# One switch and a new hand-written order in a chunk-attention and token-mixing kernel: every transpose of x and u on TensorE

## The chip, the cores and the metric

The kernel runs on one core of one Trainium2 chip. The metric is device time in microseconds (us), the median of several runs. One core has five engines with queues of their own: TensorE (PE, matmuls; PEld are its weight loads), VectorE (DVE), ScalarE (ACT), GpSimd (POOL) and SyncE (SP). In this kernel POOL computes almost nothing: it issues DMAs, and so does SP.

## The reference

```python
# q, k, v: (8 batches, 8 heads, 576 tokens, 64), float32
scores = q_chunk @ k_chunk.T / sqrt(64)          # 9 chunks of 64 tokens, each on its own
attn   = softmax(scores)
x      = attn @ v_chunk                          # -> (8, 576, 512), heads side by side

theta  = x @ w_theta                             # 512 x 512
zr, zi = x * cos(theta), x * sin(theta)
y      = w_tok_r @ zr + w_tok_i @ zi             # 576 x 576, over the tokens of a batch
u      = x + y
out    = u + relu(u @ w_ch)                      # 512 x 512
```

## The kernel before

The 8 batches are taken in 4 pairs (p = 0 to 3). The 1152 tokens of a pair are 9 tiles of 128 (the middle one takes 64 tokens of each batch), and for attention these are 5 groups g of 2, 2, 1, 2 and 2 tiles. Groups 0 and 1 belong to the pair's first batch, 3 and 4 to its second, group 2 to both. Work is cut into steps, and a list written out by hand, `ORDER`, says in which order the steps are emitted. Each engine and each DMA queue runs its own instructions strictly in that order, so a step whose input is late holds up everything behind it on its engine. The steps, with p and g or another index behind the dot, and after the colon bits that choose engines:

- Loads, all issued from POOL: `lq` (q and k of a group, one DMA of 256 KB each, L165), `lv` (v, 2 or 3 DMAs, L186), `lw` and `lc` (w_theta, w_ch, L203), `lt.half.ri` (a part of a token weight, L194 and L199).
- `a1`: 32 PE transposes of q and k (L277) and two copies out of PSUM, one behind the other (L208 on DVE, L210 on ACT). `a2`: scores (L303) and their exponential on ACT (L310). `a3`: attention times v (L331), then reciprocal and product on DVE (L338, L345); the result is x.
- `a4`: the transpose of x, which `a5` needs. Below bit 16 it is 8 PE transposes (4 for the middle group, L385) and a copy out of PSUM; with bit 16 it is DMA transposes issued from SP (L364, L360).
- `a5`: theta (L410, 8 matmuls, 4 for the middle group), then cos and sin on ACT (L420, L424). `z`: x times cos or sin on DVE (L435; the middle group has four smaller products and two small DMAs, L445 to L450).
- `tw`: PE transposes of the token weights (L229). `yh` and `y`: token mixing, 18 matmuls each (L467 in quarters for the first batch of all, L488 for the others), and u = x + y on DVE (L475, L496). They leave u transposed, in `uT`.
- `w.p.j`: u @ w_ch for one of 9 tiles, 4 matmuls (L519). For the final sum u must be turned back. In the first `U_DMA` batches `w` does this with 4 more matmuls against the identity (L527), ACT takes the relu (L535) and DVE adds (L542). In the later ones step `ut` has turned u by DMA transposes from SP (L510), and one DVE instruction does relu and sum (L544).
- `st.p.j`: that DVE instruction, and the output DMA (L554) from POOL (bit 2) or SP.

PSUM results go through 4 buffers in turn, so a PE step must wait until the evacuation of the step four places earlier is done.

```python
if 2 * p + int(j >= KT) < U_DMA:        # in w (L526, L533) and in out_tile (L541)
if bits & 16:                           # in a4 (L376)
    xt(p, g)                            # dma_start_transpose on SP
```

Of the kernel before, what the change touches and what calls it, by code (L numbers as in the profile page):

```python
# [16 lines left out]


ORDER = """
lq.0.0:0 a1.0.0:2 lq.0.2:0 a1.0.2:2 lq.0.1:0 a2.0.0:0 a2.0.2:0 a1.0.1:3 lv.0.2:0  # L20
lv.0.0:0 a3.0.0.0:0 a3.0.2.0:0 a2.0.1:0 a3.0.0.1:0 lv.0.1:0 a3.0.1.0:0 lw.0:0 lq.0.3:0
a3.0.1.1:0 a4.0.0:1 a4.0.2:0 lq.0.4:0 a4.0.1:1 a5.0.2:0 lt.0.1:0 z.0.2.0:0 a5.0.0:0
lt.0.0:0 z.0.0.0:0 a1.0.3:3 a5.0.1:0 lq.1.0:0 a1.0.4:0 z.0.1.0:0 lv.0.4:0 tw.0.2:0
tw.0.0:0 z.0.1.1:0 lt.1.0:0 z.0.0.1:0 tw.0.1:0 a2.0.3:0 lt.1.1:0 a2.0.4:0 lv.0.3:0
lv.1.0:0 a1.1.0:2 yh.0.0:0 lq.1.2:0 a3.0.4.0:0 a2.1.0:0 a3.0.4.1:0 yh.0.1:0 a4.0.4:1
lc.0:0 tw.1.1:0 tw.1.2:1 tw.1.0:1 a3.0.3.0:0 lq.1.1:0 a3.0.3.1:0 a5.0.4:0 lv.1.2:0
a4.0.3:1 yh.1.0:0 lq.1.3:0 a5.0.3:0 z.0.4.0:0 lq.1.4:0 a3.1.0.0:0 z.0.3.0:0 a1.1.2:2
yh.1.1:0 z.0.3.1:0 z.0.4.1:0 a2.1.2:0 lv.1.3:0 a3.1.0.1:0 a1.1.1:3 lv.1.1:0 w.0.0:0
st.0.0:0 y.0.1.0:0 a3.1.2.0:0 a1.1.3:0 lq.2.0:0 w.0.1:0 lv.1.4:0 a4.1.2:1 st.0.1:0
y.0.1.1:0 a2.1.3:0 a1.1.4:3 a2.1.1:0 a3.1.3.0:0 lq.2.2:0 w.0.2:0 st.0.2:0 y.0.1.2:0  # L30
a2.1.4:0 a3.1.3.1:0 a4.1.0:1 a5.1.2:0 lv.3.0:0 a3.1.1.0:0 a1.2.0:2 a5.1.0:0 lq.2.1:0
lv.2.2:0 a3.1.4.0:0 lv.2.0:0 a3.1.1.1:0 y.0.1.3:0 a4.1.1:1 a3.1.4.1:0 z.1.0.0:0 a1.2.2:1
w.0.3:0 st.0.3:0 a4.1.3:1 a4.1.4:0 lq.2.3:0 z.1.2.0:0 a5.1.1:0 w.0.4:0 a5.1.4:0 st.0.4:2
w.0.5:0 lq.2.4:0 z.1.1.0:0 z.1.0.1:0 z.1.4.0:0 a5.1.3:0 st.0.5:0 z.1.1.1:0 a2.2.0:0
a1.2.1:2 y.1.0.0:0 lv.2.1:0 a1.2.3:1 a3.2.0.0:0 lv.2.4:0 z.1.3.0:0 a2.2.2:0 y.1.0.1:0
z.1.3.1:0 a2.2.1:0 lv.3.2:0 a3.2.2.0:0 a1.2.4:0 w.0.6:0 st.0.6:0 a4.2.2:1 lv.2.3:0
y.1.0.2:0 w.0.7:0 z.1.4.1:0 a3.2.0.1:0 lq.3.0:0 a2.2.4:0 st.0.7:2 lv.3.4:0 y.1.0.3:0
a3.2.1.0:0 a3.2.4.0:0 y.1.1.0:0 a4.2.0:0 a3.2.4.1:0 a1.3.0:3 a2.2.3:0 lq.3.2:0
a3.2.1.1:0 w.0.8:0 lq.3.1:0 lq.3.3:0 a5.2.2:0 a4.2.1:0 lv.3.3:0 w.1.0:0 lq.3.4:0
st.0.8:0 lv.3.1:0 z.2.2.0:0 st.1.0:0 y.1.1.1:0 a5.2.1:0 w.1.1:0 st.1.1:2 a5.2.0:0  # L40
z.2.1.0:0 z.2.0.0:0 y.1.1.2:0 a3.2.3.0:0 a1.3.2:0 z.2.1.1:0 a2.3.0:0 a1.3.1:0 z.2.0.1:0
w.1.2:0 st.1.2:0 y.1.1.3:0 y.2.0.0:0 ut.1.1.0:0 a2.3.2:0 ut.1.1.3:0 a3.3.0.0:0 a1.3.3:0
a3.2.3.1:0 y.2.0.1:0 a4.2.4:16 a4.2.3:17 a2.3.1:0 a3.3.0.1:0 a1.3.4:0 a2.3.3:0
a3.3.1.0:0 ut.1.1.2:0 y.2.0.2:0 a3.3.1.1:0 a4.3.0:17 a2.3.4:0 ut.2.0.1:0 ut.1.1.1:0
a3.3.3.0:0 a5.2.3:0 w.1.3:0 a5.2.4:0 st.1.3:2 y.2.0.3:0 z.2.3.0:0 w.1.4:0 a4.3.1:17
a5.3.0:0 z.2.3.1:0 st.1.4:2 z.2.4.0:0 z.2.4.1:0 w.1.5:0 st.1.5:2 z.3.0.0:0 a5.3.1:0
w.1.6:0 st.1.6:0 y.2.1.0:0 a3.3.4.0:0 a3.3.2.0:0 ut.2.0.0:0 ut.2.0.2:0 y.2.1.1:0
a3.3.4.1:0 a3.3.3.1:0 z.3.1.0:0 w.1.7:0 st.1.7:2 y.2.1.2:0 ut.2.0.3:0 w.1.8:0 a4.3.2:18
a5.3.2:0 a4.3.3:17 z.3.0.1:0 a4.3.4:17 st.1.8:2 w.2.0:0 st.2.0:2 z.3.2.0:0 z.3.1.1:0
y.2.1.3:0 a5.3.3:0 z.3.3.0:0 w.2.1:0 ut.2.1.1:0 ut.2.1.3:0 a5.3.4:0 st.2.1:0 w.2.2:0  # L50
ut.2.1.0:0 ut.2.1.2:0 st.2.2:2 y.3.0.0:0 w.2.3:0 st.2.3:2 y.3.0.1:0 w.2.4:0 st.2.4:2
y.3.0.2:0 z.3.3.1:0 ut.3.0.1:0 ut.3.0.2:0 ut.3.0.0:0 w.2.5:0 z.3.4.0:0 z.3.4.1:0
st.2.5:0 y.3.0.3:0 w.2.6:0 ut.3.0.3:0 st.2.6:2 y.3.1.0:0 w.2.7:0 st.2.7:0 y.3.1.1:0
w.2.8:0 st.2.8:2 ut.3.1.1:0 ut.3.1.0:0 y.3.1.2:0 w.3.0:0 st.3.0:2 y.3.1.3:0 w.3.1:0
st.3.1:2 w.3.2:0 w.3.3:0 ut.3.1.2:0 ut.3.1.3:0 w.3.4:0 st.3.2:0 st.3.3:2 st.3.4:0
w.3.5:0 st.3.5:0 w.3.6:0 st.3.6:0 w.3.7:0 w.3.8:0 st.3.7:0 st.3.8:2
""".split()


# [1 line left out]
def kernel(  # L61
# [28 lines left out]
    VP = D + 2  # L90
    NAT = 7

    U_DMA = 3

    const = ctx.enter_context(tc.tile_pool(name="const", bufs=1))
    glob = ctx.enter_context(tc.tile_pool(name="glob", bufs=1))
# [104 lines left out]
    def load_w(ap, f16):  # L201

        nc.gpsimd.dma_start(f16, ap.rearrange("(a p) e -> p a e", p=P))  # L203
# [38 lines left out]
    st = {}  # L242
# [271 lines left out]
    def w(p, j):  # L514
# [3 lines left out]
        for db in range(NDB):  # L518
# [6 lines left out]
            )  # L525
            if 2 * p + int(j >= KT) < U_DMA:  # L526
                nc.tensor.matmul(  # L527
# [4 lines left out]
        r = None  # L532
        if 2 * p + int(j >= KT) < U_DMA:  # L533
            r = outp.tile([P, DM], FP32, name="relu", bufs=3)
# [3 lines left out]
    def out_tile(p, j, bits):  # L538
        ps, r = st[p].pop(("w", j))
        o = outp.tile([P, DM], FP32, name="o32")  # L540
        if 2 * p + int(j >= KT) < U_DMA:  # L541
            nc.vector.tensor_tensor(out=o, in0=ps[:, DM : 2 * DM], in1=r, op=ALU.add)  # L542
# [10 lines left out]
        for pp, bb, s0, n in out_ranges(j):  # L553
# [4 lines left out]
                st=out_tile, tw=tw, ut=ut, lq=load_qk, lv=load_v, lt=load_tok_w,  # L558
                lw=lambda _: load_w(moe_w_theta, wtheta16),
                lc=lambda _: load_w(moe_w_ch, wch16))  # L560
# [38 lines left out]
```

## Time and profile before

| | |
|---|---|
| Time, median of 3 runs | 211.57 us (211.16 to 212.69) |
| The profiled run | 212.69 us, of which the traced span is 210.7 us |
| PE busy | 190.6 us (90%), 2850 matmuls |
| DVE, ACT, POOL busy | 131.7, 97.4, 96.7 us |
| Mean granted TensorE clock | 0.982 |
| DMA | 31.63 MB; transposes: 12 of x for whole tiles, 1 for a middle tile, 20 of u |

PE is the engine to look at, but its busy share alone doesn't tell what an added or removed matmul costs: matmuls overlap, so one lasts longer than the distance to the next. The distance is read from the chain of waits, where each piece starts when the one before lets it. Times inside the trace count from the start of the span.

### The profile page before, as it was taken

The numbers are of one execution on the slowest core, as the hardware profiler recorded it, in microseconds if no ns is written. First come the engines' busy times: TensorE is split into PE (matmuls) and PEld (weight loads), VectorE is DVE, ScalarE is ACT, GpSimd is POOL, SyncE is SP. The second block draws the span as 40 slices with busy tenths as digits, with TensorE's granted clock in tenths as the row PEclk, the third lists the DMA queues.
The fourth block names the chain that finished last, engine by engine and source line by source line (L and its number), as shares of the span: only waits on it lengthen the run. The fifth ranks groups of instructions, "written<-read, shape, count | busy, mean of one in ns | idle before, by whom it ended". The sixth has DMA issues, their size and how long they took to land.

```text
span 210.7 us, 6454 instructions
## 1 busy us (share of the span) xinstructions
PE 190.6 (90%) x2850; PEld 130.8 (62%) x2850; DVE 131.7 (63%) x230; ACT 97.4 (46%) x106; POOL 96.7 (46%) x139
## 2 busy tenths in 40 slices
PE   0657998999999999999999999969999999999980
PEld 0546567767787674686766588834567647667530
DVE  0338688758947986776876376741659854664660
ACT  2042895467265768973276864665460342000000
POOL 7999446797597911975599300000120302211211
PEclk9999999999999999999999999997999999999996
DMA  5999999999999993999999996665354796462883
GB/s 50 166 157 179 190 193 189 137 155 173 168 196 201 151 164 83 150 162 115 170 101 156 224 180 82 91 84 106 101 155 88 183 156 171 124 176 68 193 279 136
DMA packets 101947, 31.63 MB, mean 150 GB/s; under 512 B 95776, under 2 KB 98464, under 8 KB 101920
## 3 DMA queue, kind: packets, MB, share of 16 engines
q0 software_dynamic: 79184, 21.26, 96.9%
q1 hardware_dynamic: 22736, 9.97, 21.5%
q8 instruction: 22, 0.36, 0.7%
q14 instruction: 5, 0.04, 0.1%
HBM read 33.06 MB, written 9.44 MB: 202 GB/s over the span
## 4 chain that ended last, share of the span: by engine, by line
PE 64%; issue 11%; POOL 10%; DMA 8%; ACT 2%; DVE 2%; POOLq 0%; SPq 0%
PE ps_y L488 22%; PE ps_theta L410 12%; PE ps_uw L519 9%; DMA qk<-in_k_dram 6%; PE ps_qkT L277 6%; POOL qk L165 5%; PE ps_y L467 4%; PE ps_sT L303 3%; POOL v L186 3%; PE ps_x L331 3%; DMA xT<-x 2%; PE ps_xT L385 2%; POOL out_dram L554 2%; PE ps_uw L527 1%; ACT qT L210 1%
## 5 line engine op out<-in xcount | busy, mean ns | idle before, releaser
L488 PE MATMUL ps_y<-wT,z 128*128 128x288 f16 x448 | 59.5, 286 | 0.1
L554 POOL DMA_DIRECT2D out_dram<-o x21 | 11.5, 550 | 89.4 <-DVE o L544 50.3
L488 PEld LDWEIGHTS <-z 128*128 128x128 f16 x448 | 43.0, 98 | 14.0 <-issue 0.2
L186 POOL DMA_DIRECT2D v<-in_v_dram x56 | 41.9, 776 | 12.8 <-DMA qk<-in_k_dram 8.1
L519 PE MATMUL ps_uw<-wch,uT 128*128 128x512 f16 x144 | 39.0, 386 | 0.0
L496 DVE TENSOR_TENSOR uT<-ps_y,xT 128x576 f16<-128x576 f32 x28 | 21.1, 756 | 22.1 <-PE ps_y L488 22.1
L410 PE MATMUL ps_theta<-wtheta,xT 128*128 128x512 f16 x128 | 31.2, 386 | 1.9 <-DMA xT<-x 1.9
L420 ACT ACTIVATE cos<-ps_theta,pihalf 128x1024 f16<-128x1024 f32 (+1 forms) x20 | 20.6, 1029 | 19.6 <-PE ps_theta L410 19.0
L310 ACT ACTIVATE eT<-ps_sT 128x1024 f16<-128x1024 f32 (+1 forms) x20 | 18.6, 939 | 23.2 <-PE ps_sT L303 23.1
L277 PE MATMUL ps_qkT<-id,qk 128*64 128x128 f16 (+1 forms) x640 | 22.6, 227 | 6.9 <-DMA qk<-in_q_dram 5.9
L345 DVE TENSOR_TENSOR x<-ps_x,recip 128x512 f16<-128x512 f32 x36 | 24.9, 692 | 1.2
L277 PEld LDWEIGHTS <-qk 128*64 128x64 f16 (+1 forms) x640 | 19.1, 118 | 9.4 <-DMA qk<-in_q_dram 5.9
L519 PEld LDWEIGHTS <-uT 128*128 128x128 f16 x144 | 14.2, 99 | 15.0 <-issue 1.1
L410 PEld LDWEIGHTS <-xT 128*128 128x128 f16 x128 | 12.0, 99 | 15.7 <-DMA xT<-x 2.4
L165 POOL DMA_DIRECT2D qk<-in_q_dram x24 | 19.6, 821 | 2.5 <-PE ps_x L331 1.5
L165 POOL DMA_DIRECT2D qk<-in_k_dram x24 | 19.5, 814 | 1.4 <-DMA qk<-in_k_dram 0.8
L542 DVE TENSOR_TENSOR o<-ps_uw,relu 128x512 f32<-128x512 f32 x13 | 8.9, 687 | 16.4 <-ACT relu L535 16.3
L544 DVE SCALAR_TENSOR_TENSOR o<-ps_uw,un 128x512 f32<-128x512 f32 x23 | 15.9, 689 | 5.2 <-PE ps_uw L519 3.6
L424 ACT ACTIVATE sin<-ps_theta 128x1024 f16<-128x1024 f32 (+1 forms) x20 | 18.6, 930 | 0.0
L208 DVE COPY kT<-ps_qkT 128x1024 f16<-128x1024 f16 (+1 forms) x11 | 13.1, 1191 | 7.5 <-ACT qT L210 7.5
L210 ACT COPY kT<-ps_qkT 128x1024 f16<-128x1024 f16 (+1 forms) x9 | 10.6, 1181 | 9.5 <-DVE qT L208 9.5
L331 PE MATMUL ps_x<-v,eT 64*64 64x65 f16 x576 | 11.4, 200 | 3.4 <-DMA v<-in_v_dram 2.5
(52 smaller groups left out, 205.7 us busy)
## 6 DMA issues: line engine op xcount, KB each, us to landing
out_dram<-o SPq DMA_DIRECT2D x17, 256.0 KB, 2.6
qk<-in_q_dram POOLq DMA_DIRECT2D x16, 256.0 KB, 6.6
qk<-in_k_dram POOLq DMA_DIRECT2D x16, 256.0 KB, 7.3
out_dram<-o POOLq DMA_DIRECT2D x15, 256.0 KB, 2.8
v<-in_v_dram POOLq DMA_DIRECT2D x40, 64.0 KB, 6.3
v<-in_v_dram POOLq DMA_DIRECT2D x16, 128.0 KB, 6.2
out_dram<-o POOLq DMA_DIRECT2D x6, 128.0 KB, 2.5
wnat<-in_moe_w_tok_i_dram POOLq DMA_DIRECT2D x2, 288.0 KB, 9.0
```

The source lines that it names most:

```text
L165: nc.gpsimd.dma_start(t[(pp // 2) : (pp // 2) + m // 2, ti].rearrange("p h t d -> p h (t d)"), src.rearrange("h (p t) d -> p h (t d)", t=2),)
L186: nc.gpsimd.dma_start(v16[pp : pp + m, sl, :, 0:D], v[2 * p + bb, :, s0 : s0 + m, :].rearrange("h s d -> s h d"),)
L277: nc.tensor.transpose(psv[par * D : par * D + D, w, e, tk, 0:rows], t[0:rows, w, 2 * e + par, tk, :], id16[0:rows, 0:rows],)
L310: nc.scalar.activation(out=eT[:, 0:n].rearrange("p i e r c -> p r (i e) c"), in_=psv[:, :, 0:n].rearrange("p r i e c -> p r (i e) c"), fun ...
L331: nc.tensor.matmul(psv[half * CH : half * CH + CH, kh if n == 2 else f0, cols], eT[kh * CH : kh * CH + CH, i, h // 2, h % 2, :], v16[kh * ...
L345: nc.vector.tensor_tensor(out=xo, in0=px[:, :, :, 0:D], in1=recip.broadcast_to((P, 2, NE, D)), op=ALU.mult,)
L410: nc.tensor.matmul(ps[:, jj * DM : jj * DM + DM], xt[:, db, :], wtheta16[:, db, :], start=(db == 0), stop=(db == NDB - 1),)
L420: nc.scalar.activation(out=cos[:, 0:n].rearrange("p a e -> p (a e)"), in_=pin, func=AF.Sin, bias=pihalf, scale=1.0,)
L424: nc.scalar.activation(out=sin[:, 0:n].rearrange("p a e -> p (a e)"), in_=pin, func=AF.Sin)
L488: nc.tensor.matmul(psv[:, hf, 0:HS], zt[:, db * P : db * P + P], wT[:, kt, hf * HS : hf * HS + HS], start=(kt == 0), stop=(kt == 2 * KT),)
L496: nc.vector.tensor_tensor(out=uT_tile(p)[:, db, sl].rearrange("p (f c) -> p f c", f=2), in0=psv[:, :, 0:HS], in1=xT_tile(p)[:, db, sl].rea ...
L519: nc.tensor.matmul(ps[:, 0:DM], uT[:, db, j * P : j * P + P], wch16[:, db, :], start=(db == 0), stop=(db == NDB - 1),)
```

## The change

It sets `U_DMA` to 8 and replaces the whole of `ORDER`. With `U_DMA` at 8, all 8 batches take the identity matmuls, the relu on ACT and the sum on DVE; the new list has no `ut` step and no `a4` with bit 16. The loads come in another order too.

```diff
 ORDER = """
-lq.0.0:0 a1.0.0:2 lq.0.2:0 a1.0.2:2 lq.0.1:0 a2.0.0:0 a2.0.2:0 a1.0.1:3 lv.0.2:0
-lv.0.0:0 a3.0.0.0:0 a3.0.2.0:0 a2.0.1:0 a3.0.0.1:0 lv.0.1:0 a3.0.1.0:0 lw.0:0 lq.0.3:0
-a3.0.1.1:0 a4.0.0:1 a4.0.2:0 lq.0.4:0 a4.0.1:1 a5.0.2:0 lt.0.1:0 z.0.2.0:0 a5.0.0:0
-lt.0.0:0 z.0.0.0:0 a1.0.3:3 a5.0.1:0 lq.1.0:0 a1.0.4:0 z.0.1.0:0 lv.0.4:0 tw.0.2:0
-tw.0.0:0 z.0.1.1:0 lt.1.0:0 z.0.0.1:0 tw.0.1:0 a2.0.3:0 lt.1.1:0 a2.0.4:0 lv.0.3:0
-lv.1.0:0 a1.1.0:2 yh.0.0:0 lq.1.2:0 a3.0.4.0:0 a2.1.0:0 a3.0.4.1:0 yh.0.1:0 a4.0.4:1
...
-w.0.3:0 st.0.3:0 a4.1.3:1 a4.1.4:0 lq.2.3:0 z.1.2.0:0 a5.1.1:0 w.0.4:0 a5.1.4:0 st.0.4:2
-w.0.5:0 lq.2.4:0 z.1.1.0:0 z.1.0.1:0 z.1.4.0:0 a5.1.3:0 st.0.5:0 z.1.1.1:0 a2.2.0:0
...
-a3.2.3.1:0 y.2.0.1:0 a4.2.4:16 a4.2.3:17 a2.3.1:0 a3.3.0.1:0 a1.3.4:0 a2.3.3:0
...
+lq.0.0:0 a1.0.0:0 lq.0.2:0 lq.0.1:0 a1.0.2:3 a2.0.0:0 lv.0.0:0 a1.0.1:3 a3.0.0.0:0
+lv.0.2:0 a2.0.2:0 a2.0.1:0 lv.0.1:0 a3.0.2.0:0 a3.0.0.1:0 lw.0:0 lt.0.1:0 a3.0.1.0:0
+a4.0.2:0 a4.0.0:0 lq.0.3:0 a3.0.1.1:0 a5.0.2:0 tw.0.1:0 a4.0.1:0 z.0.2.0:0 a5.0.0:0
+a1.0.3:2 a5.0.1:0 z.0.0.0:0 z.0.0.1:0 lt.0.0:0 lq.0.4:0 tw.0.2:0 z.0.1.0:0 tw.0.0:1
+lt.1.0:0 a2.0.3:0 z.0.1.1:0 lv.0.3:0 a1.0.4:3 lt.1.1:0 tw.1.0:0 yh.0.0:0 lq.1.0:0
...
+w.0.3:0 st.0.3:0 a4.1.1:1 a4.1.2:3 y.0.1.2:0 a2.1.4:0 a3.1.3.0:0 a3.1.3.1:0 a5.1.2:0
+a5.1.1:0 y.0.1.3:0 a4.1.3:0 a3.1.4.0:0 a1.2.0:3 a3.1.4.1:0 lq.2.1:0 z.1.1.0:0 a1.2.2:1
+w.0.4:0 lv.2.3:0 lv.2.0:0 lq.2.3:0 lv.2.2:0 a5.1.0:0 st.0.4:0 z.1.2.0:0 z.1.0.0:0
+a4.1.4:0 w.0.5:0 lv.2.1:0 a1.2.1:3 w.0.6:0 st.0.5:0 a5.1.4:0 z.1.1.1:0 st.0.6:2
+z.1.4.0:0 w.0.7:0 z.1.0.1:0 lq.2.4:0 lv.2.4:0 z.1.4.1:0 a5.1.3:0 st.0.7:0 z.1.3.0:0
+y.1.0.0:0 a2.2.2:0 lq.3.0:0 a2.2.0:0 a2.2.1:0 y.1.0.1:0 w.0.8:0 z.1.3.1:0 st.0.8:2
...
+st.3.4:0 w.3.5:0 w.3.6:0 st.3.5:0 st.3.6:0 w.3.7:0 w.3.8:0 st.3.7:2 st.3.8:2
 """.split()
...
-    U_DMA = 3
+    U_DMA = 8
```

On PE the instruction list grows from 5702 to 5990 rows: 144 matmuls and their 144 weight loads, 92 of them L527's (52 to 144) and 52 L385's (92 to 144). On ACT there are 23 more relus. SP loses its 33 transposes and keeps 8 small DMAs and its outputs.

## The prediction

> **What bounds the kernel now.** I read the slices first, to see where TensorE stands still, then the chain of waits for what one more PE instruction costs, then the groups by line and the stage windows for the engines beside it.
>
> ```profile
> PE   0657998999999999999999999969999999999980
> PEclk9999999999999999999999999997999999999996
> ```
>
> A slice is 5.3 us. PE is short of work in the first six slices (to about 33 us) and in the last; between them only slice 27 shows a hole, and there the clock falls too. So from 33 to 204 us the end is set by the PE list, and a PE instruction added there is paid in full unless it fills that hole. The chain gives prices as distances between starts:
>
> ```profile
> 74.91 0.45 PE ps_xT L385 x8
> ...
> 82.74 0.22 PE ps_uw L519
> 83.01 0.22 PE ps_uw L519
> 83.28 0.21 PE ps_uw L519
> 83.56 0.22 PE ps_uw L519
> 83.83 1.73 PE ps_theta L410 x8
> ...
> 136.65 0.47 SPq L364
> 137.17 4.49 DMA xT<-x
> 141.71 1.83 PE ps_theta L410 x4
> 143.54 0.43 PE ps_uw L519
> ...
> 145.51 1.73 PE ps_theta L410 x8
> ...
> 149.45 0.86 PE ps_uw L519 x4
> ```
>
> Eight transposes of x take 0.45 us, 0.056 each. A `w` with identity matmuls takes 83.83 - 82.74 = 1.09 us, one without 0.86: the four extra cost 0.23, again 0.056 each. The hole is a DMA transpose: x is ready at 136.65, lands at 141.7, and the second half of a theta step waits for it. The step's first four matmuls start at 138.78 and take 4 x 0.216, so PE was free at 139.64 and stood 2.07 us. Then the four thetas and the `w` behind them need 145.51 - 141.71 = 3.80 us instead of 0.86 + 1.09: 1.85 us more, at half clock (granted clock 0.83 in the stretch from 140 to 150, 1.00 around it).
>
> **What the change does to this, part by part.**
>
> *PE work.* 144 matmuls more (92 of L527, 52 of L385): 144 x 0.056 = +8.1 us. All of it lies after 55 us, where PE has no other idle time, so nothing covers it. The 2850 matmuls of before stay. The Trainium skill ("TensorE: Matmul & The Clock Gate", Part 4) puts a PE transpose inside a kernel at about 275 ns, and says that transposes don't count as PE work for the clock; by that the addition would be an estimated 40 us. The trace shows 219 ns of duration but 0.056 of distance, and the granted clock is 1.00 in every 10 us stretch that holds the 92 of before, so the row decides.
>
> *The hole.* The new list has no transpose on SP, so the wait goes: -2.07 and -1.85, together -3.9 us. The same page ("Why this matters for your kernels") says a clock drop takes an idle gap above some 3 us; here 2.07 us was enough. By the page the 1.85 us would have another cause and stay. The median run may not have had the drop at all (it is 1.1 us below the profiled one), so the saving is between 2.1 and 3.9 us; I take 3.9. What is late next is the PE list itself. The 20 transposes of u never stop the chain (DVE's L544 waits for L519, 3.6 us in total, not for them), so their removal gains nothing. Nor does SP's list: its other work is stores and the small `zm` DMAs.
>
> *The head.* Up to w_theta the loads come in the same order but for v. Before, the first `yh` starts at 33.53, when the eighth load behind w_theta has landed:
>
> ```profile
> 32.96 0.64 PE L277 MATMUL ps_qkT<-id,qk 128*64 128x128 f16 x16 [0.58 <-DMA qk<-in_k_dram]
> ```
>
> POOL's issues that wait for such landings one after the other stand at 21.53 and, seven loads later, at 33.20: 1.67 us per load. In the new list the first `yh` stands behind `tw.1.0`, which needs the seventh load behind w_theta and a quarter-size one: 32.96 - 1.67 + 0.4 = 31.7, plus 12 transposes of 0.056, so `yh` starts at about 32.4. That is 1.1 us earlier, with `tw.1.0` (0.6) already done, but `a1.1.0` (1.01) and `a2.0.4` (0.62) still to do: 0.1 ahead. I take 0, with one load's distance, 1.67 us, either way. The label of the change says that q and k of the second batch come ahead of the token weights; the lists show the reverse (`lt.0.1` and `lt.0.0` move up among `lq.0.3` and `lq.0.4`).
>
> *ACT in the middle.* 23 relus and 6 more copies of xT move onto ACT.
>
> ```profile
> L420 ACT ACTIVATE cos<-ps_theta,pihalf 128x1024 f16<-128x1024 f32 x16 | 17.8, 1114 | 18.2 <-PE ps_theta L410 17.6 <-ACT sin L424 0.6
> L424 ACT ACTIVATE sin<-ps_theta 128x1024 f16<-128x1024 f32 x16 | 16.3, 1016 | 0.0
> L535 ACT ACTIVATE relu<-ps_uw 128x512 f32<-128x512 f32 x13 | 7.8, 601 | 2.2 <-PE ps_uw L527 2.2
> L310 ACT ACT_TABLE_LOAD x5 | 6.4, 1283 | 0.8 <-PEq L583 0.7
> L210 ACT COPY xT<-ps_xT 128x1024 f16<-128x1024 f16 x3 | 3.0, 1012 | 4.6 <-PE ps_xT L385 4.6
> ```
>
> The tight stretch is the one with all five theta steps of pair 1, `a5.1.2` to `a5.1.3`. New list, PE: five `a5` 7.8, one `y` 2.2, four `w` 4.4, `a1` of 2.5 groups 2.5, two `a4` 0.9, two `a3` 0.5, sum 18.3 us. ACT, in the same list: table load 1.28, cos and sin 4 x 2.13 + 1.28, two xT copies 2.02, q and k copies 2.02 + 1.33, four relus 2.40, sum 18.9. So ACT outlasts PE by 0.6 us there. In the old list the same stretch is 17.1 on PE and 15.2 on ACT. And ACT was close already:
>
> ```profile
> 80.00:90.00 10.00, 10.00 (x134) 6.27 (x134) 7.09 (x12) 9.33 (x10) 6.50 (x10) 1.00 0.68 114
> ```
>
> (The columns after the stretch are its length and the busy time of PE, PEld, DVE, ACT and POOL.) Behind a late cos stand `z` on DVE, in its strict order the sums of `st` behind that, and through the four PSUM buffers the next `w` on PE. In pair 3 the same count gives 15.7 on PE and 15.5 on ACT, in pair 2 21.1 and 17.8. So PE will stand for at least the 0.6 us excess, and for more where the PSUM turn adds latency; the longest stop of the old middle is 2.07 us, and one such in each of the two tight pairs makes 4. I take 2.0 us, nearer the low end because 93% ACT cost PE nothing, and keep 0 to 4 for the range (0 if the copies' latency is hidden after all).
>
> *The tail.* Now the last sum waits for an output buffer:
>
> ```profile
> 205.24 0.69 DVE L544 SCALAR_TENSOR_TENSOR o<-ps_uw,un 128x512 f32<-128x512 f32 x1 [0.74 <-DMA out_dram<-o]
> ```
>
> With `w` 1.09 instead of 0.86 us apart, four buffers come round in 4.4 instead of 3.4 us, so this 0.74 should vanish; in its place the relu (0.60) comes between the last matmul and the sum. I set it at 0; if the buffer wait stays, +0.6. DVE's sum costs the same (687 against 689 ns).
>
> **The sum.** +8.1 - 3.9 + 0 + 2.0 + 0 = +6.2 us. Against the profiled run's own 212.69 that is 218.9, against the median of 211.57 it is 217.8; I say 218.3. Lowest from the bounds: 8.1 - 3.9 - 1.7 + 0 = +2.5, on the median 214.1. Highest: 8.1 - 2.1 + 1.7 + 4 + 0.6 = +12.3, 223.9.
>
> **Rivals.**
> 1. *PE work alone, nothing waits in the middle, the head a load earlier*: +2.5 to +4.2, 214 to 215.8. For it: no idle time on PE before in the middle with ACT at 93%. Against: the ACT sum above.
> 2. *ACT becomes the bound and a stop halves the clock again*: the 4 us of stops and another 1.85, +10 or more, above 222.
> 3. *Faster: the head shrinks.* The first 33.5 us hold about 16 us of PE work, so there is idle time to win. To be over 1% faster the kernel has to win the 4.2 us that the rest costs and 2.1 more, 6.3 us, so the first `yh` would have to start at 27 us or so with as much behind it. It decides on when `lt.0.0` lands: sixth load behind w_theta before (PE waits for it until 28.90), fourth now, about 25.6, but three more loads stand before `tw.1.0`, which comes ahead of `yh`. The time would be 209 or less; against it is that the loads follow each other at 1.67 us whatever their order.
> 4. *Within 1%*: the head wins 2 us or more, and no stops. 212 to 213.7.
> 5. *The change doesn't do what it says*: some transposes would still be on SP. The instruction lists show none, so I give this no chance.
>
> **How the numbers follow.** Forecast (215.8 to 222) 0.62; rival 1 0.18; rival 2 0.07; rival 3 0.04; rival 4 0.09. What a measurement of this kernel can tell from no change is about 1%, 2.1 us. The range 214.0 to 222.5 leaves out rivals 3 and 4 and half of rival 2, some 0.17. Faster is rival 3, 0.04. Same is rival 4 and 0.02 of rival 1, whose lowest end borders on it, 0.11. Slower is the rest, 0.85.
>
> **What would show it.** In the profile after: the two groups of transposes (L527 and L385 now) at 144 each, still 0.056 apart; no wait on xT by DMA and a granted clock of 1.00 from 22 us to the end of PE; PE idle times of 0.3 to 2 us in the theta stretch of pair 1 (between 80 and 95 us) that end with a relu, a cos or DVE's sum; the first `yh` between 31 and 34 us; the last sum started by the relu. The forecast is wrong if PE's middle has no hole (then rival 1), or if `yh` starts before 29 us (rival 3).

## The result, and the profile after

| | before | after |
|---|---|---|
| Median | 212.13 us (4 runs, 211.16 to 212.75) | 219.48 us (4 runs, 219.19 to 222.64) |
| Ratio, with 95% interval | | 1.035 (1.029 to 1.041) |
| Profiled run, its span | 212.69, 210.7 | 219.19, 217.4 |

The kernel became slower by 7.4 us on the medians and by 6.5 between the profiled runs. (Some runs of several kernels, before included, came out more than 1.5% above the fastest of the same kernel; the ratios leave those out, and e5 to e8 have no ratio because one run of before is left beside them.) The slices of the profile after (5.4 us each) show PE full from the eighth slice to the last but one, without the hole, at full clock:

```profile
PE   0678978999999999999999999999999999999990
PEclk9999999999999999999999999999999999999999
```

The groups by line (count behind the x, then busy us and mean ns of one) show the added work at about the durations of before (L527 224 ns, L385 239, the relu 601): 144 matmuls of each kind, and 36 relus.

```profile
L532 ACT ACTIVATE relu<-ps_uw 128x512 f32<-128x512 f32 x36 | 21.6, 604 | 34.4 <-PE ps_uw L524 34.3
L524 PE MATMUL ps_uw<-id,uT 128*128 128x128 f16 x144 | 31.5, 219 | 0.0
L382 PE MATMUL ps_xT<-id,x 128*128 128x128 f16 x144 | 11.6, 227 | 0.3 <-DVE x L342 0.3
```

In the timeline of PE between 79 and 89 us, the theta stretch of pair 1, two instructions wait (start us, us, instruction, and in brackets the idle time before it and what ended it):

```profile
80.93 1.89 PE L407 MATMUL ps_theta<-wtheta,xT 128*128 128x512 f16 x8 [0.49 <-DVE kT L205]
88.57 0.38 PE L516 MATMUL ps_uw<-wch,uT 128*128 128x512 f16 x1 [0.29 <-DVE kT L205]
```

Both wait for a PSUM buffer that DVE's copy of k has to leave, of `a1.2.0` and of `a1.2.1`, and that copy follows the copy of q on ACT. The timeline of all engines shows what stood ahead of the first stop:

```profile
77.41 1.08 PE L274 MATMUL ps_qkT<-id,qk 128*64 128x128 f16 x32
78.54 1.50 ACT L207 COPY qT<-ps_qkT 128x1024 f16<-128x1024 f16 x2 [0.26 <-PE ps_qkT L274]
79.58 1.30 DVE L205 COPY kT<-ps_qkT 128x1024 f16<-128x1024 f16 x1 [1.11 <-ACT qT L207]
```

Nothing on ACT made that one late: ACT stood idle for 0.26 us until the transposes had ended at 78.49, and copied q at once (the first of the two copies in that line). The stop is the length of the two copies, one behind the other, 1.0 us on ACT and 1.3 on DVE. It is different ahead of the second stop, in the timeline of ACT:

```profile
83.87 1.01 ACT L421 ACTIVATE sin<-ps_theta 128x1024 f16<-128x1024 f32 x1
84.77 1.01 ACT L207 COPY xT<-ps_xT 128x1024 f16<-128x1024 f16 x1
85.66 0.62 ACT L532 ACTIVATE relu<-ps_uw 128x512 f32<-128x512 f32 x1
86.15 1.03 ACT L207 COPY qT<-ps_qkT 128x1024 f16<-128x1024 f16 x1
87.04 0.64 ACT L532 ACTIVATE relu<-ps_uw 128x512 f32<-128x512 f32 x1
```

The transposes of `a1.2.1` end at 85.36. Their q copy on ACT starts at 86.15, behind a sin, a copy of xT and a relu. DVE copies k from 87.22 to 88.52, and PE goes on with `w.0.7` at 88.57. (So the buffer is that of the step three places back, not four: the sum that empties the buffer of `w.0.5` ends only at 89.08.)

To compare kernels I use one sum for all. Each step of the PE list is counted at its distance (`y` 2.21, a group of `a5` 1.73, `w` 1.09 or 0.86, eight transposes 0.45 and so on). The start of a step less the count of all steps before it is what PE has lost by then, to idle time or a low clock. The counts are chosen, so the levels of the columns are less firm than the differences between rows. I read it at `yh.1.1` (47 to 51 us, the end of the head) and at the last `w`. The four columns add up to the span, all in us, from the profiled runs:

| | PE work before the last `w` | lost by `yh.1.1` | lost after it | last `w` to the end | span |
|---|---|---|---|---|---|
| before | 180.7 | 18.0 | 4.9 | 7.1 | 210.7 |
| after | 188.6 | 19.0 | 2.7 | 7.1 | 217.4 |
| e1, u on PE | 185.7 | 18.8 | 1.1 | 7.4 | 212.9 |
| e2, x on PE | 183.6 | 19.8 | 3.1 | 7.1 | 213.5 |
| e3, all on PE, old order | 188.6 | 18.2 | 3.1 | 7.4 | 217.3 |
| e4, `y` moved | 180.7 | 18.7 | 4.7 | 7.0 | 211.1 |
| e5, identity twice | 196.4 | 21.6 | 2.1 | 7.4 | 227.5 |
| e6, new order, u by DMA | 183.6 | 19.3 | 5.9 | 8.3 | 217.1 |
| e8, new with old head | 188.6 | 18.5 | 3.4 | 7.1 | 217.6 |
| e10, x before u on SP | 180.7 | 18.0 | 1.1 | 7.0 | 206.9 |
| e11, e3 with `a4.3.2` early | 188.6 | 19.3 | 2.0 | 7.4 | 217.2 |
| e13, q copies on DVE | 188.6 | 21.7 | 1.8 | 7.2 | 219.2 |

So between the two kernels: +7.9 of work (and 0.2 in the last `w`), +1.0 in the head, -2.2 behind it. The -2.2 is the hole of before, 3.8, less 1.6 of other stops; 1.1 of the 1.6 are the two stops above.

### The profile page after: what moved, and what is told of

It is laid out like the page before. It is cut to its first block, busy times and chain, and to the rows that moved or that the text cites. A ratio compares the mean times of both kernels' runs of the same rounds, so it can differ in the third digit from the quotient of the medians.

```text
span 217.4 us, 6716 instructions
## 1 busy us (share of the span) xinstructions
PE 198.5 (91%) x2994; PEld 138.5 (64%) x2994; DVE 129.0 (59%) x223; ACT 121.0 (56%) x143; POOL 93.6 (43%) x133
## 4 chain that ended last, share of the span: by engine, by line
issue 51%; POOL 20%; PE 18%; ACT 4%; DMA 3%; DVE 3%; POOLq 0%; ACTq 0%
POOL v L183 8%; POOL qk L162 8%; PE ps_theta L407 5%; POOL out_dram L551 3%; PE ps_y L485 3%; DMA v<-in_v_dram 3%; PE ps_y L464 2%; PE ps_qkT L274 2%; PE ps_xT L382 1%; PE ps_sT L300 1%; PE ps_uw L516 1%; PE ps_x L328 1%; ACT cos L417 1%; ACT kT L207 1%; PE ps_wT L226 1%
## 5 line engine op out<-in xcount | busy, mean ns | idle before, releaser
L551 POOL DMA_DIRECT2D out_dram<-o x15 | 8.4, 557 | 104.4 <-DVE o L539 104.4
L516 PE MATMUL ps_uw<-wch,uT 128*128 128x512 f16 x144 | 42.4, 380 | 0.3 <-DVE kT L205 0.3
L532 ACT ACTIVATE relu<-ps_uw 128x512 f32<-128x512 f32 x36 | 21.6, 604 | 34.4 <-PE ps_uw L524 34.3
L524 PE MATMUL ps_uw<-id,uT 128*128 128x128 f16 x144 | 31.5, 219 | 0.0
L407 PE MATMUL ps_theta<-wtheta,xT 128*128 128x512 f16 x128 | 30.1, 379 | 0.7 <-DVE kT L205 0.5
L539 DVE TENSOR_TENSOR o<-ps_uw,relu 128x512 f32<-128x512 f32 x36 | 24.6, 686 | 9.4 <-ACT relu L532 9.2
L205 DVE COPY kT<-ps_qkT 128x1024 f16<-128x1024 f16 (+1 forms) x10 | 12.4, 1242 | 14.7 <-ACT qT L207 14.7
L421 ACT ACTIVATE sin<-ps_theta 128x1024 f16<-128x1024 f32 (+1 forms) x20 | 18.7, 937 | 0.0
L207 ACT COPY kT<-ps_qkT 128x1024 f16<-128x1024 f16 (+1 forms) x10 | 11.4, 1141 | 12.4 <-DVE qT L205 12.4
```

The source lines that it names most:

```text
L407: nc.tensor.matmul(ps[:, jj * DM : jj * DM + DM], xt[:, db, :], wtheta16[:, db, :], start=(db == 0), stop=(db == NDB - 1),)
L516: nc.tensor.matmul(ps[:, 0:DM], uT[:, db, j * P : j * P + P], wch16[:, db, :], start=(db == 0), stop=(db == NDB - 1),)
L524: nc.tensor.matmul(ps[:, DM + db * P : DM + db * P + P], uT[:, db, j * P : j * P + P], id16,)
L532: nc.scalar.activation(out=r, in_=ps[:, 0:DM], func=AF.Relu)
```

## The experiments

### e1: only u on PE

```diff
-    U_DMA = 3
+    U_DMA = 8
```

and the 20 `ut` steps leave the old list.

> The old order with U_DMA at 8: the steps that turn u by DMA (ut) are left out of the list, x of the last groups still goes by DMA. Theory A (PE's list is the bound, each added identity matmul is paid at its distance of 0.056 us): 92 more L527 matmuls, 5.2 us, and the hole at 139.4 us with its half clock stays, so the time is that of before + 5.2, a ratio near 1.024. Theory B (the relu on ACT and the two-step sum are what costs): more than + 6, with PE idle times that end with a relu or a DVE sum. Theory C (the new order of work and loads is what costs): within 1% of before.

Measured: 214.94 us against 211.51, ratio 1.016 (1.008 to 1.023). That is below what theory A asked, and the table says why: the work came (+5.0), but the loss after the head went from 4.9 to 1.1. The hole is gone, though x still goes by DMA: from `a5.2.3` to `y.2.0.3`, the stretch with the hole, PE takes 8.29 us before and 4.54 in e1. The chain of waits of e1 goes through the theta step without a stop, from 139.58 on at full clock:

```profile
139.46 0.12 PE ps_x L328 x14
139.58 1.86 PE ps_theta L407 x8
141.45 0.22 PE ps_uw L516
```

### e2 and e3: x on PE, and all on PE, in the old order

e2 takes bit 16 from all seven `a4` steps that have it; e3 does that and what e1 does.

```diff
-a4.2.4:16 a4.2.3:17 a4.3.0:17 a4.3.1:17 a4.3.2:18 a4.3.3:17 a4.3.4:17
+a4.2.4:0 a4.2.3:1 a4.3.0:1 a4.3.1:1 a4.3.2:2 a4.3.3:1 a4.3.4:1
```

> The old order with bit 16 taken from all a4 steps: x goes through PE everywhere, u still goes by DMA in the last five batches. Theory A: 52 more L385 matmuls, + 2.9 us, and the hole goes, - 3.9 where the clock dropped and - 2.1 where it did not: between - 1.0 and + 0.8, ratio 0.995 to 1.004, and no wait for xT by DMA. Theory B or C: the DMA transposes of x were worth nothing or were a loss, so - 2 or better.

> The old order with both: no ut, U_DMA at 8, no bit 16. It does the same work as the changed kernel, in the old order. Theory A: + 8.1 - 3.9 = + 4.2 us, ratio near 1.020, PE idle as before up to 139 us; what the changed kernel has on top, some 2.5 us, is then the price of the new order (1.0 at the head, 1.4 in the middle, as the two traces have it). If the order costs nothing the time is that of the changed kernel, ratio 1.035; if the order is all (theory C), the time of before.

Measured: e2 214.69 us, ratio 1.015 (1.007 to 1.023); e3 219.63 us, ratio 1.038 (1.031 to 1.046). Both lie above theory A, and e3 is as slow as the changed kernel. In the profiled run of e2, 1.8 us of that lie in the head (19.8 against 18.0). In both a new stop came in, here in the PE timeline of e3:

```profile
164.47 0.39 PE L382 MATMUL ps_xT<-id,x 128*128 128x128 f16 x4
165.80 1.04 PE L407 MATMUL ps_theta<-wtheta,xTm 128*128 128x512 f16 x4 [0.94 <-ACT xTm L207]
```

The old order has `a4.3.2` directly ahead of `a5.3.2`. By DMA that costs PE nothing, since SP runs ahead of PE: in the trace of before it issues that transpose at 161.7, and it lands at 164.1, 0.7 us before the step starts. On PE, the four transposes are followed at once by the step that needs them, and it waits for the copy out of PSUM (in e3 1.1 us of loss there, and 0.5 at the `w` behind it, which waits for a sin). An order made for one route carries over to the other at a price.

### e4: other work ahead of the step that waits

```diff
-a5.2.3:0 w.1.3:0 a5.2.4:0 st.1.3:2 y.2.0.3:0
+y.2.0.3:0 a5.2.3:0 w.1.3:0 a5.2.4:0 st.1.3:2
```

> The old kernel with one step moved: y.2.0.3 (18 matmuls, 2.2 us) ahead of a5.2.3, the theta step that waits 2.07 us for x by DMA. If the hole is a stop of PE's list that other ready work can fill, it goes and the half clock after it too: - 2.1 to - 3.9 us, ratio 0.982 to 0.990, granted clock 1.00 from 22 us on. If the hole is a limit of the DMA transposes themselves, it moves to the next theta step and the time stays within 0.5% of before.

Measured: 211.87 us (10 runs), ratio 1.005 (1.002 to 1.008): nothing gained. The stop at 139 is gone, and the PE timeline shows the same wait at later theta steps, at 151 and again at 171 us:

```profile
150.78 1.04 PE L410 MATMUL ps_theta<-wtheta,xT 128*128 128x512 f16 x4 [0.69 <-DMA xT<-x]
171.25 1.04 PE L410 MATMUL ps_theta<-wtheta,xT 128*128 128x512 f16 x4 [1.07 <-DMA xT<-x]
```

So it is not one late tile: with the first wait filled, later transposes of x are late. e4 doesn't say whether there are too many DMA transposes or whether they stand in a bad order; e10 does.

### e5: the identity matmuls twice

```diff
+                for _ in range(2):
                     nc.tensor.matmul(
                         ps[:, DM + db * P : DM + db * P + P],
```

> The changed kernel with each identity matmul of w issued twice into the same place: 144 matmuls and 144 weight loads more, nothing else. Theory A: 144 x 0.056 = + 8.1 us over the changed kernel, ratio to before near 1.073, and PE's idle time as in the changed kernel. Theory B (ACT and DVE behind PE set the pace): less than + 4, since PE would only fill time in which it stood.

Measured: 230.02 us (227.4 to 231.8). In the table the work rose by 7.8 (and 0.2 in the last `w`), and the loss behind the head fell from the 2.7 of the changed kernel to 2.1: the stop at `w.0.7` is gone and the other one of pair 1 is shorter (0.27 us of waiting instead of 0.49). So of 8.0 us added, 0.6 filled time in which PE stood, and 7.4 were paid. The other 2.6 us of its span were lost in the head, which e13 comes back to.

### e6: the new order with u by DMA

`U_DMA` back to 3, and a `ut` step behind each `y` of the last five batches.

```diff
-y.3.0.0:0 w.2.6:0 st.2.5:2 y.3.0.1:0
+y.3.0.0:0 ut.3.0.0:0 w.2.6:0 st.2.5:2 y.3.0.1:0 ut.3.0.1:0
```

> The changed kernel's order with U_DMA back at 3, and a ut step behind each y of the last five batches; x stays on PE. Theory A: 92 matmuls fewer, - 5.2 us against the changed kernel, ratio to before near 1.010, if the 20 transposes on SP land in time for the sums. Theory B: more than - 5.2, since 23 relus leave ACT too and the stops of the middle (1.4 us) shrink. If SP's transposes hold up its output stores, less than - 4.

Measured: 221.99 us (219.1 to 224.2), and the traced span is 217.1 against 217.4: no gain over the changed kernel. PE has 5.0 us less to do, but lost 3.2 more behind the head and 1.2 more at the end. DVE waited 5 us for one transpose of u, and PE behind it for the PSUM buffer; the timelines of DVE and of PE:

```profile
169.74 0.69 DVE L544 SCALAR_TENSOR_TENSOR o<-ps_uw,un 128x512 f32<-128x512 f32 x1 [5.04 <-DMA un<-uT]
```

```profile
170.49 0.61 PE L385 MATMUL ps_xT<-id,x 128*128 128x128 f16 x8 [2.12 <-DVE o L544]
```

### e7 and e13: two copies from ACT to DVE

```diff
-a1.2.0:3
+a1.2.0:2
-a1.2.1:3
+a1.2.1:2
```

> The changed kernel with two engine bits changed: the q copies of a1.2.0 and a1.2.1 go from ACT to DVE (bits 3 to 2). In the changed kernel PE stops 0.65 us at 80.2 and 0.45 us at 88.0 until DVE's kT copy of these steps, which waits for their q copy on ACT, behind relus, cos, sin and xT copies. If ACT's fullness in that stretch is the cause, both stops go: - 1.1 us. If it is DVE or the PSUM turn as such, they stay or move, within 0.3 us.

> e7 again (the q copies of a1.2.0 and a1.2.1 on DVE in the changed kernel), since e7's time was disturbed at the head: both stops of the theta stretch stay away, and 1.1 us less than the changed kernel's own run beside it. If the time is that of the changed kernel, the two stops are paid back later.

Measured: e7 221.56 us (218.5 to 222.0), e13 the same kernel 219.72 us (218.1 to 221.1), beside 222.54 us (219.2 to 223.3) for the changed kernel itself in e12. The times scatter too much to show 1 us. The trace of e13 does. In its PE timeline the theta steps `a5.1.0` and `a5.1.4` start without a wait in brackets, and so does `w.0.7` behind the latter:

```profile
83.16 1.90 PE L407 MATMUL ps_theta<-wtheta,xT 128*128 128x512 f16 x8
88.63 1.89 PE L407 MATMUL ps_theta<-wtheta,xT 128*128 128x512 f16 x8
90.36 0.38 PE L516 MATMUL ps_uw<-wch,uT 128*128 128x512 f16 x1
```

From `w.0.4` to `a5.1.0` PE takes 1.31 us instead of 1.75 (1.09 would be without a stop), from `a5.1.4` to `w.0.7` 1.73 instead of 2.18. The second stop is gone, 0.2 of the first stayed, no new one came in, and the loss behind the head fell from 2.7 to 1.8 us. The second stop was made by ACT's order, in which the q copy came late. The first was not: there the q copy had started at once, and what shortened it is that the copy takes 0.69 us on DVE and 1.01 on ACT.

### e8: the old head in front of the new order

The list is the old one up to `yh.1.1`, then what remains of the new one, in its order.

> The changed kernel with the old list up to yh.1.1 (loads and work), and behind it what is left of the new list in its order. By the traces PE has lost 1.0 us more than before when yh.1.1 starts: if that is the new head's own price, the time is 1.0 us below the changed kernel, ratio to before near 1.030. If the head's loss is taken back later by loads that stand ready sooner, no difference; if the old head leaves later loads late, PE stops for v or q after 50 us.

Measured: 219.50 us (219.28 to 219.88), the median of the changed kernel. The head lost 0.5 us less, and a wait of 0.94 us for v came in at 59 us: in this trace what the old head gives is taken back by a later load.

```profile
59.28 0.32 PE L328 MATMUL ps_x<-v,eT 64*64 64x65 f16 x15 [0.94 <-DMA v<-in_v_dram]
```

### e10: x ahead of u on SP

```diff
-w.1.2:0 st.1.2:0 y.1.1.3:0 y.2.0.0:0 ut.1.1.0:0 a2.3.2:0 ut.1.1.3:0 a3.3.0.0:0 a1.3.3:0
-a3.2.3.1:0 y.2.0.1:0 a4.2.4:16 a4.2.3:17
+w.1.2:0 st.1.2:0 y.1.1.3:0 y.2.0.0:0 a2.3.2:0 a3.3.0.0:0 a1.3.3:0
+a3.2.3.1:0 y.2.0.1:0 a4.2.4:16 a4.2.3:17 ut.1.1.0:0 ut.1.1.3:0
```

> The old kernel with two ut steps (ut.1.1.0 and ut.1.1.3, DMA transposes of u on SP) moved behind a4.2.4 and a4.2.3 (four DMA transposes of x on SP), nothing on PE changed. Theory D, new after e1: the hole is SP's queue; its transposes follow each other at some 1.3 us, x of group 2.3 is ready at 132.2 but two transposes of u stand in front, and with u on PE the same x transposes landed by 138.8 instead of 141.7. By it the hole goes: - 2.1 us, and - 3.9 in runs in which the clock dropped; ratio 0.982 to 0.992, faster than both kernels. Theory E, the transposes of x are slow by themselves and PE waits for whichever comes late: the stop stays at a5.2.3 or moves to a theta step behind, ratio 0.997 to 1.005.

Measured: 209.98 us (12 runs) against 212.11, ratio 0.994 (0.990 to 0.997). It is faster than both kernels, by 0.6% than before, with 1 outside the interval (all runs taken, the medians lie 2.1 us apart). The ratio lies just above the span that theory D gave (0.982 to 0.992), so the median run of before has less of a hole than its profiled one. The SP timeline of before and then of e10:

```profile
129.05 3.17 SPq L510 DMA_TRANSPOSE un<-uT  x2
132.27 6.16 SPq L364 DMA_TRANSPOSE xT<-x  x4
138.48 2.50 SPq L510 DMA_TRANSPOSE un<-uT  x1
```

```profile
129.02 6.05 SPq L364 DMA_TRANSPOSE xT<-x  x4
135.12 4.48 SPq L510 DMA_TRANSPOSE un<-uT  x3
```

SP needs 1.2 to 2.5 us per transpose, whichever tensor it takes. With two of u in front, the four of x were issued from 132.3 to 138.4, and the last landed at 141.7. With x in front they were issued by 135.1 and, by the trace's landing events, all there at 138.1, ahead of the theta step that starts at 138.78. The chain of e10 runs on without a stop:

```profile
138.66 0.12 PE ps_x L331 x16
138.78 1.86 PE ps_theta L410 x8
140.65 0.22 PE ps_uw L519
```

The stretch from `a5.2.3` to `y.2.0.3` takes 4.54 us instead of 8.29, and the loss behind the head is 1.1 instead of 4.9, with the same work on PE and the same 33 transposes on SP. So their order was at fault, not their number.

In the trace of before the x that came late was complete long before its last transpose was issued at 137.17: DVE's product of `a3.2.3.1` ends at 132.24.

```profile
131.55 0.69 DVE L345 TENSOR_TENSOR x<-ps_x,recip 128x512 f16<-128x512 f32 x1
```

### e11: e3 with the middle tile's transposes earlier

```diff
-w.1.8:0 a4.3.2:2 a5.3.2:0
+a4.3.2:2 w.1.8:0 a5.3.2:0
```

> e3 (old order, all transposes on PE) with the middle tile's transposes a4.3.2 one step earlier, ahead of w.1.8. In e3 they stand directly before a5.3.2, and PE stopped 1.1 + 0.5 us there for the copies out of PSUM and behind them. If that is e3's only price of using an order made for DMA transposes, - 1.6 us against e3, 2 us faster than the changed kernel: then the new order costs 2 us of the changed kernel's 7.4. If the stop moves, the time of e3 and of the changed kernel.

Measured: 218.74 us (218.6 to 219.2), ratio 1.032 (1.027 to 1.038), 0.9 below e3's median where 1.6 was expected; the stop of 1.1 is gone and the 0.5 behind it stayed. In the profiled runs the spans are 217.2 and 217.3, because the head of e11 lost 1.1 more.

### e12: the changed kernel again

> The changed kernel as it is, on the same chip as the runs beside it: + 7.4 us over before, ratio 1.035. It says whether e11's and e13's distances to it are their own or the chip's.

Measured: 222.54 us (219.2 to 223.3), ratio 1.042 (1.032 to 1.051), which rests on two of its runs, 219.2 and 222.3. The kernel scatters on this chip. Beside it e11 is about 1% faster and e13 about 0.5%, with intervals that overlap; beside the first comparison e11 is 0.7 us faster and e13 0.2 slower. So neither distance is settled by the times.

## Why the prediction was right, and where a reason was not

The forecast of 218.3 us (214.0 to 222.5), slower with 0.85, stands against 219.48. By its steps:

- *PE work, +8.1*: 7.9 up to the last `w` and 0.2 in it. e5 adds as much again and pays 7.4 of it; the distance of 0.056 us per transpose held. The 275 ns of the Trainium skill ("TensorE: Matmul & The Clock Gate", Part 4) are said of the transpose mode of TensorE. Only the 52 of L382 are written as `nc.tensor.transpose`, while the 92 of L524 are plain matmuls against the identity, so the estimate of 40 us by that page went too far, and by the page it would be an estimated 14 us for the 52. The clock stayed at 1.00 behind the head with all 288 of them in the kernel, but other matmuls always stand between them, so no run here shows whether transposes alone would keep it up.
- *The hole, -3.9*: 3.8 in the profiled run. On the medians it is less: e10 removes the hole with PE's list unchanged, and gains 0.6%, 1.3 us. I had put the change between 2.1 and 3.9 and taken the upper end, which is the step that was mis-sized for the median.
- *"The 20 transposes of u never stop the chain, so their removal gains nothing. Nor does SP's list"*: this step failed. The wait of PE carried x's name, and I took the route of x for the cause. I also read 136.65 as the moment at which x is ready; it is the moment at which SP turns to the last transpose of it. This x was complete at 132.24 (the product shown in e10) and stood in SP's queue from then on. e1 left x on the DMA route and took u off it, and the hole went; e10 changed only which of the two stands first on SP, and it went too. Two transposes of u, each harmless for its own consumer, stood in front of x's. That the number was not hurt is luck: the change removes both kinds.
- *The head, 0 with 1.67 either way*: `yh` starts at 32.31, where 32.4 was worked out, but two stops behind it (the scores of group 4 wait for a copy, then `yh.0.1`) make +1.0 in the profiled run. e8, with the old head, has the same median as the changed kernel.
- *ACT in the middle, +2.0*: by the traces 1.6, of which the two stops of pair 1 are 1.1 in losses (0.66 and 0.45); the rest are small stops that were not traced one by one. The place was right, the reason only in part. The stops end with the k copy of an `a1` step, not with a relu, a cos or DVE's sum as I had said. Only the smaller one has the cause that I gave, ACT with too much ahead in its list; it held up a q copy, and e13 takes it away. The larger one, 0.66, came with ACT idle just before it: there the two copies one behind the other are longer than the PSUM turn allows. That the sum comes near 2.0 is partly luck.
- *The tail, 0*: 7.1 us from the last `w` to the end in both. The last sum now waits for the relu, as worked out, and no longer for a buffer:

```profile
212.21 0.69 DVE L539 TENSOR_TENSOR o<-ps_uw,relu 128x512 f32<-128x512 f32 x1 [0.40 <-ACT relu L532]
```

What the new order costs for itself is small, and its size is not settled: the old order with all transposes on PE has a span of 217.3 us (e3) or 217.2 (e11) against 217.4, while the times put e11 between 0.7 us and some 1% below the changed kernel. The 7.4 us are mostly the transposes on PE: e3, which changes them and keeps the old order, has the ratio 1.038 where the change has 1.035.

How often the stop of before halves the clock, the mean granted clock of its other runs says in part. Each stretch at half clock that lies between two at full clock lasts 3.41 us or twice that in the traces, and 3.41 us at half take 0.8% off the mean clock of a run of 211 us. So a run with 0.993 or more had no such drop, and 12 of the 20 runs of before that the ratios of e1 and e10 use are of this kind. That fits a hole worth less on the median than in the profile. How long PE stands in these runs stays open: the stop itself is in no record but the one trace.

## What to carry to other kernels

Price an added instruction by its distance to the next in the chain, and check whether the engine has idle time behind it: here 144 small transposes at 0.056 us each moved onto a full engine and added their whole sum of 8 us to its list. When a wait names a DMA, look at what stands ahead of it in the issuing queue, whoever it belongs to, before giving up the route: here moving two steps back in SP's list removed the same wait at no cost that the trace shows, where moving the transposes to PE cost 8 us of its time. And an order made for a transfer that nobody waits for has to be spread out again when the same work moves onto an in-order engine, since a step and its consumer may then stand side by side.

## What the hardware showed that I had not expected

The new order's head is not the same in each execution. In four profiles that have it PE had lost 19.0, 19.3, 21.6 and 21.7 us at `yh.1.1` (after, e6, e5, e13); with the old head it was 18.0 to 19.8 in eight. In e13 PE waits 1.72 us ahead of the scores of group 4, where it waits 0.54 in the changed kernel's first trace, and 1.1 us later the clock drops to half for 3.41 us; the timeline of PE, and the windows of e13 (length, busy time of PE, PEld, DVE, ACT and POOL, granted clock, DMA):

```profile
36.33 0.69 PE L300 MATMUL ps_sT<-qT,kT 64*64 64x64 f16 x32 [1.72 <-DVE kT L205]
```

```profile
34.00:37.00 3.00, 1.28 (x52) 0.85 (x50) 2.02 (x3) 0.95 (x2) 2.99 (x5) 1.00 1.92 175
37.00:41.00 4.00, 3.71 (x37) 2.75 (x33) 2.18 (x5) 1.02 (x1) 2.02 (x5) 0.57 2.41 150
```

So, as in the hole of before (2.07 us of standing, then half clock), stops well below the 3 us of the Trainium skill ("TensorE: Matmul & The Clock Gate", "Why this matters for your kernels") were followed by a drop. But not each does it: in e6 PE waits 2.12 us at 168 to 170 us and the granted clock stays at 1.00. What decides between the two, no run here shows.
